# The last stores of an attention and feed-forward kernel: one transfer for each 128-row quarter, and the last quarter scaled in two halves

## The chip, the cores and the metric

The kernel runs on one core of a Trainium2 chip. The metric is the time of one execution in microseconds on the device; the median of several runs is compared. A core has a matrix engine (TensorE, PE in the profile), a vector engine (VectorE, DVE), a scalar engine (ScalarE, ACT), GpSimd (POOL) and SyncE (SP), which mainly issues transfers. Each engine runs its own instructions in order and waits on semaphores for the others. Transfers between the on-chip memory (SBUF) and the device memory (DRAM) are issued by SyncE, ScalarE or GpSimd and carried out by 16 DMA engines that all queues share. Matrix products are accumulated in PSUM, eight banks of 2 KB for each of 128 partitions; VectorE and ScalarE read them from there.

## The reference

Attention over 32 memory slots for 8 batches and 8 heads, then a bilinear feed-forward layer. Cut to what matters:

```python
# attention: q, k, v (8, 8, 576, 64), phi (8, 8, 576, 32)
a = softmax(phi, axis=2)
k_m = einsum('bhsm,bhsd->bhmd', a, k)
v_m = einsum('bhsm,bhsd->bhmd', a, v)
attn_out = softmax(q @ k_m.T / 8) @ v_m

# feed-forward: x (4608, 512), w_a, w_b (512, 1536), w_out (1536, 512)
x = attn_out.transpose(0, 2, 1, 3).reshape(4608, 512)
out = ((x @ w_a) * (x @ w_b)) @ w_out          # float32, (4608, 512)
```

## The kernel before, in words

The 4608 tokens are handled as 36 blocks of 128 rows; a block consists of two slots of 64 rows. A row of a slot is one token, and the tokens of one slot stand nine rows apart in the output (`out_rows`, with `NI` = 9 slots in a batch). Two neighbouring slots of one batch stand one row apart.

A long hand-written list, `PLAN`, sets the order in which the parts of the attention, the two upward products (`up_half`, which writes the products a * b into `ht`) and the downward product are recorded; each engine executes its instructions in that order. There is no scheduler behind it. The downward product with `w_out` is in `two_downs`: two blocks at a time, by Strassen's scheme (Winograd's form), with seven products of six matmuls each in place of eight. The sums of token blocks (`h_sums`, line 537) and of weight blocks (`w_sums`) are made beforehand by VectorE and GpSimd. A generator yields after each matmul, so that the plan can mix these steps with others; at the very end only they are left.

For the two blocks of one call there are two output tiles of 128 x 512 in SBUF, `o1` and `o2`. Each has a right half (columns 256 to 511) and a left half (columns 0 to 255), which gives four quarters. They become ready in this order:

1. `o1` right: product into bank `pv`, then `plus` (VectorE, line 564) scales it and adds `u2`
2. `o2` right: product into bank `py`, then `plus`
3. `o1` left: product into a bank of its own, `px`, then `plus`
4. `o2` left: product `a22` times `T4` into `py`, then only a scaling

`part` (ScalarE, line 560) makes the scaled partial sums `u1`, `u5` and `u2`.

The last call (`ends`, where `cidx` is `BLOCKS - 2`) differs from the others. The others scale the fourth quarter on ScalarE (line 604) and store each block whole, one transfer for each slot, from SyncE. The last call scales the fourth quarter on VectorE (line 602) and stores each quarter as soon as it is ready, in two transfers of 64 rows x 256 columns (64 KB, rows of 1 KB), one for each slot. `store` (lines 539 to 543) takes the two engines that issue them:

- `o1` right: both on GpSimd (line 583)
- `o2` right: SyncE and ScalarE (line 588)
- `o1` left: SyncE and ScalarE (line 595)
- `o2` left: SyncE and ScalarE (line 606)

An issue waits on its engine for the quarter that it sends, and blocks what stands behind it on that engine. After the last store the program ends: SyncE waits for the semaphores of all transfers, and a barrier of all engines follows.

Of the kernel before, what the change touches and what calls it, by code (L numbers as in the profile page):

```python
# [11 lines left out]
ALU = mybir.AluOpType  # L12
# [66 lines left out]
def kernel(  # L79
# [11 lines left out]
    nc = tc.nc  # L91
# [3 lines left out]
    d_model, d_ff = moe_w_a.shape  # L95
    NHP = H // 2
    NI = S // 64
# [408 lines left out]
    out_rows = out.rearrange("(b p i) f -> b i p f", b=B, i=NI)  # L506

    KH = NFF // 2
    NH = d_model // 2
    w_sums = wpool.tile([P, 4, KH, NH], F16, name="w_sums")  # L510

    def quarter(x, y):
        return wo_sb[:, KH * x:KH * (x + 1), NH * y:NH * (y + 1)]
# [8 lines left out]
    def tokens_of(cidx, x):  # L522
        pair, c = divmod(cidx, NI)
        return ht[:, KH * x:KH * (x + 1), P * c:P * (c + 1)]
# [13 lines left out]

    def store(o_sb, cidx, cs=slice(0, d_model), engines=(nc.sync, nc.sync)):
        pair, c = divmod(cidx, NI)  # L540
        for z in range(2):
            slot = 2 * c + z
            engines[z].dma_start(out=out_rows[2 * pair + slot // NI, slot % NI, :, cs], in_=o_sb[64 * z:64 * z + 64, cs])

    def two_downs(cidx):
        T1, T2, T3, T4 = (w_sums[:, x] for x in range(4))
        (a11, a12), (a21, a22) = ([tokens_of(cidx + y, x) for x in range(2)] for y in range(2))
        scale = 1.0 / (CS * CS)
        ends = cidx == BLOCKS - 2

        def products(po, lhs, rhs, first=False):
            for i in range(KH):
                nc.tensor.matmul(po, lhs[:, i], rhs[:, i], start=first and i == 0,  # L553
                                 stop=i == KH - 1, skip_group_check=not first)
                if i < KH - 1:
                    yield

        def part(po, name):
            x = ppool.tile([P, NH], F32, name=name)
            nc.scalar.mul(out=x, in_=po, mul=scale)  # L560
            return x

        def plus(o, po, x):
            nc.vector.scalar_tensor_tensor(out=o, in0=po, scalar=scale, in1=x, op0=ALU.mult, op1=ALU.add)

        o1, o2 = (opool.tile([P, d_model], F32, name="o_sb") for _ in range(2))
        y, ybank = banks.take([P, NH], F32, "py", hold=True)
        yield from products(y, a11, quarter(0, 0), True)
        u1 = part(y, "u1")
        yield  # L570
        v, vbank = banks.take([P, NH], F32, "pv", hold=True)
        S1, S2, S4, S3 = (h_sums[cidx][:, x] for x in range(4))
        yield from products(v, S1, T1, True)
        u5 = part(v, "u5")
        yield
        yield from products(y, S2, T2)
        u2 = part(y, "u2")
        yield
        yield from products(v, S4, quarter(1, 1))
        banks.free(vbank)  # L580
        plus(o1[:, NH:], v, u2)
        if ends:
            store(o1, cidx, slice(NH, d_model), (nc.gpsimd, nc.gpsimd))
        yield
        yield from products(y, S3, T3)
        plus(o2[:, NH:], y, u5)
        if ends:
            store(o2, cidx + 1, slice(NH, d_model), (nc.sync, nc.scalar))
        yield
        x, xbank = banks.take([P, NH], F32, "px", hold=True)  # L590
        yield from products(x, a12, quarter(1, 0), True)
        banks.free(xbank)
        plus(o1[:, :NH], x, u1)
        if ends:
            store(o1, cidx, slice(0, NH), (nc.sync, nc.scalar))
        else:
            store(o1, cidx)
        yield
        yield from products(y, a22, T4)
        banks.free(ybank)  # L600
        if ends:
            nc.vector.tensor_scalar(out=o2[:, :NH], in0=y, scalar1=scale, scalar2=None, op0=ALU.mult)
        else:
            nc.scalar.mul(out=o2[:, :NH], in_=y, mul=scale)
        if ends:
            store(o2, cidx + 1, slice(0, NH), (nc.sync, nc.scalar))
        else:
            store(o2, cidx + 1)
        yield
# [3 lines left out]
    def downs():  # L613
        for cidx in range(0, BLOCKS, 2):
            yield from two_downs(cidx)
# [19 lines left out]
    for x in PLAN.split():  # L635
# [17 lines left out]
        elif x[0] in "hg":  # L653
            n, y = arg.split(".")
# [34 lines left out]
```

## Time and profile before

| what | value |
|---|---|
| median of 3 runs | 236.83 us (236.87, 236.83, 236.38) |
| the profiled execution's own time | 236.16 us |
| its span on the core | 234.4 us |
| TensorE clock granted | 0.996 of full speed |
| transfers in the span | 38420 packets, 37.27 MB |
| stores of 128 KB, issue to landing (median of 68) | 2.6 us |
| stores of 64 KB, issue to landing (median) | SyncE 2.1 us, ScalarE 2.6 us, GpSimd 2.3 us |
| GpSimd's issue of a 64 KB store | 0.58 to 0.59 us |
| SyncE's issue of a 64 KB store | 0.47 us |
| ScalarE's issue of a 64 KB store | 0.55 to 0.73 us |

The span is the time from the first to the last instruction on the core; the execution's own time holds a little more around it. The rows of busy time by slice show TensorE at 9 tenths or more nearly all the way, up to the last of 40 slices:

```profile
PE   7887899999999999999999999999999999999993
...
DMA  6999999999999998597997589853170323122155
GB/s 230 239 252 203 207 207 206 229 235 257 213 224 289 202 240 196 130 229 118 190 183 169 111 137 227 164 110 77 26 166 3 92 50 92 45 48 51 41 137 134
```

One digit is the busy share of a slice of 5.9 us in tenths. The last slice holds the end of the last products, all the quarter stores and the closing of the program. Lines of the profile read as: line of the code, engine, operation, tile written, tile read, shapes, count, and then busy time in us and the mean of one in ns. In a timeline the first two numbers are start and duration in us.

### The profile page before, as it was taken

Reading aid. Unit: us, or ns where it says so; the run is one execution under the profiler, and the core shown is the slowest. Engines: PE = TensorE matmul, PEld = TensorE weight load, DVE = VectorE, ACT = ScalarE, POOL = GpSimd, SP = SyncE. Lnnn points to the kernel's source line nnn. Section 1 sums busy time; section 2 is a strip of 40 time slices with the busy share of each in tenths; the row PEclk is TensorE's granted clock in tenths of the full one; section 3 lists DMA queues with packets and bytes.
Section 4 is the critical chain, followed back from the end, with each engine's and each line's share of the span. In section 5 each row is a group of like instructions: output and inputs, shape, how many; then the busy total and the mean of one; then the engine's idle time right before and its main releaser. Section 6 shows DMA issues by size and latency. Waiting matters only on the chain.

```text
span 234.4 us, 7699 instructions
## 1 busy us (share of the span) xinstructions
PE 224.6 (96%) x3059; PEld 169.9 (72%) x3059; DVE 185.0 (79%) x450; ACT 152.3 (65%) x398; POOL 120.0 (51%) x109
## 2 busy tenths in 40 slices
PE   7887899999999999999999999999999999999993
PEld 4533456788868886777777778888668878888882
DVE  3533889999998889868797998977978897776862
ACT  2228699875778797766687786556786865465330
POOL 7577423795779525908947982324066002325051
PEclk9999999999999999999999999999999999999998
DMA  6999999999999998597997589853170323122155
GB/s 230 239 252 203 207 207 206 229 235 257 213 224 289 202 240 196 130 229 118 190 183 169 111 137 227 164 110 77 26 166 3 92 50 92 45 48 51 41 137 134
DMA packets 38420, 37.27 MB, mean 159 GB/s; under 512 B 14672, under 2 KB 32464, under 8 KB 38384
## 3 DMA queue, kind: packets, MB, share of 16 engines
q0 software_dynamic: 19248, 23.14, 53.6%
q1 hardware_dynamic: 18624, 12.85, 23.8%
q10 hardware_dynamic: 512, 0.79, 1.0%
q8 instruction: 24, 0.39, 0.7%
q14 instruction: 12, 0.10, 0.1%
HBM read 42.47 MB, written 9.44 MB: 221 GB/s over the span
## 4 chain that ended last, share of the span: by engine, by line
PE 77%; DMA 17%; POOL 3%; issue 1%; DVE 0%; POOLq 0%
PE py L553 19%; PE pa L624 18%; PE pb L624 18%; DMA kv_sb<-in_v_dram 12%; PE pv L553 10%; PE pva L449 5%; PE px L553 5%; DMA phi_sb<-in_phi_dram 5%; PE pkv L286 2%; POOL q_sb L150 1%; PE pscore L380 1%; POOL h_sums L537 1%; POOL phi_sb L138 0%; PE pk L345 0%; POOL kv_sb L145 0%
## 5 line engine op out<-in xcount | busy, mean ns | idle before, releaser
L631 DVE TENSOR_TENSOR ht<-a_sb,pb 128x288 f16<-128x288 f16 x192 | 79.9, 447 | 18.7 <-PE pb L624 9.0
L628 ACT CAST a_sb<-pa 128x288 f16<-128x288 f32 x192 | 71.5, 408 | 34.8 <-PE pa L624 28.9
L624 PEld LDWEIGHTS <-vab 128*128 128x128 f16 x768 | 73.5, 98 | 19.6 <-issue 4.5
L624 PE MATMUL pa<-A,vab 128*128 128x288 f16 x384 | 69.9, 286 | 0.9 <-DVE A L414 0.8
L624 PE MATMUL pb<-A,vab 128*128 128x288 f16 x384 | 70.5, 286 | 0.0
L553 PEld LDWEIGHTS <-h_sums 128*128 128x128 f16 x432 | 41.6, 98 | 10.4 <-issue 3.2
L537 POOL TENSOR_TENSOR h_sums<-ht 128x768 f16<-128x768 f16 x17 | 27.9, 1646 | 29.9 <-DVE ht L631 29.9
L553 PEld LDWEIGHTS <-ht 128*128 128x128 f16 x324 | 31.3, 98 | 6.3 <-issue 1.1
L553 PE MATMUL py<-w_sums,h_sums 128*128 128x256 f16 x216 | 35.2, 273 | 0.0
L462 ACT CAST vab<-pva 128x512 f16<-128x512 f32 (+1 forms) x60 | 31.6, 568 | 4.8 <-PE pva L449 4.1
L537 POOL TENSOR_TENSOR h_sums<-h_sums,ht 128x768 f16<-128x768 f16 x12 | 19.7, 1642 | 27.3 <-DVE h_sums L537 15.9
L462 DVE CAST vab<-pva 128x512 f16<-128x512 f32 (+1 forms) x44 | 26.8, 633 | 3.4 <-PE pva L449 3.1
L537 POOL TENSOR_TENSOR h_sums<-ht,h_sums 128x768 f16<-128x768 f16 x9 | 15.0, 1664 | 17.6 <-DVE h_sums L537 17.2
L260 ACT ACTIVATE exp_sb<-phi_sb 128x576 f16<-128x576 f32 x16 | 11.0, 698 | 12.4 <-DMA phi_sb<-in_phi_dram 12.4
L560 ACT ACTIVATE u<-py 128x256 f32<-128x256 f32 x36 | 14.1, 392 | 6.9 <-PE py L553 6.5
L553 PE MATMUL py<-wo_sb,ht 128*128 128x256 f16 x108 | 18.5, 273 | 0.0
L553 PE MATMUL pv<-wo_sb,h_sums 128*128 128x256 f16 x108 | 18.5, 273 | 0.0
L553 PE MATMUL px<-wo_sb,ht 128*128 128x256 f16 x108 | 18.4, 273 | 0.0
L553 PE MATMUL pv<-w_sums,h_sums 128*128 128x256 f16 x108 | 17.7, 273 | 0.0
L553 PE MATMUL py<-w_sums,ht 128*128 128x256 f16 x108 | 17.0, 272 | 0.0
L269 DVE STREAM_TRANSPOSE qT<-q_sb 128x288 f32<-128x288 f32 x32 | 14.0, 458 | 1.8 <-DMA q_sb<-in_q_dram 1.6
L211 PE MATMUL pw<-warm 128*128 128x128 f16 (+1 forms) x67 | 12.2, 334 | 1.3 <-DVE warm L180 1.3
(67 smaller groups left out, 241.4 us busy)
## 6 DMA issues: line engine op xcount, KB each, us to landing
out_dram<-o_sb SPq DMA_DIRECT2D x68, 128.0 KB, 2.6
phi_sb<-in_phi_dram POOLq DMA_DIRECT2D x8, 576.0 KB, 7.6
kv_sb<-in_v_dram POOLq DMA_DIRECT2D x8, 576.0 KB, 10.1
kv_sb<-in_k_dram POOLq DMA_DIRECT2D x7, 576.0 KB, 12.7
q_sb<-in_q_dram POOLq DMA_DIRECT2D x6, 576.0 KB, 8.3
wo_sb<-in_moe_w_out_dram POOLq DMA_DIRECT2D x6, 256.0 KB, 15.8
q_sb<-in_q_dram POOLq DMA_DIRECT2D x4, 288.0 KB, 9.9
wa_sb<-in_moe_w_a_dram POOLq DMA_DIRECT2D x2, 512.0 KB, 14.5
```

The source lines that it names most:

```text
L211: nc.tensor.matmul(pw[:, :cols], warm[:, :P], warm[:, :cols], start=True, stop=True)
L260: nc.scalar.activation(out=t["exp"][:, 2 * z:2 * z + 2, :, :], in_=phis[b][:, 2 * z:2 * z + 2, :].rearrange("p c (i m) -> p c i m", m=M), ...
L269: nc.vector.transpose(out=t["qT"][:, hp, :].bitcast(F32), in_=qs[b][:, hp, :].bitcast(F32))
L286: nc.tensor.matmul(t["pkv"][g][0][32 * j:32 * j + 32, 0:n], t["exp"][64 * r:64 * r + 64, hp, i, :], kvs[b][64 * r:64 * r + 64, 0:3 - given ...
L449: nc.tensor.matmul(t["pva", lo, z][g][0][32 * j:32 * j + 32, 0:hi - lo], t["kvT"][64 * r:64 * r + 64, 4 + g, M * j:M * j + M], w_sbs[z][64 ...
L462: engine_copy(out=vabs[b][z][:, g, lo:hi], in_=pva[:, 0:hi - lo])
L537: engine.tensor_tensor(out=out, in0=in0, in1=in1, op=op)
L553: nc.tensor.matmul(po, lhs[:, i], rhs[:, i], start=first and i == 0, stop=i == KH - 1, skip_group_check=not first)
L560: nc.scalar.mul(out=x, in_=po, mul=scale)
L624: nc.tensor.matmul(ps, vabs[b][x][:, g, P * i:P * (i + 1)], attn[b][:, g, HALF * hf:HALF * (hf + 1)], start=(g == 0), stop=(g == 1))
L628: nc.scalar.copy(out=a_sbs[b, i, hf], in_=ps)
L631: nc.vector.tensor_tensor(out=ht[:, i, t0:t0 + HALF], in0=a_sbs.pop((b, i, hf)), in1=ps, op=ALU.mult)
```

## The change

`store` gets a form for one engine: where `engines` has one entry, it sends the whole 128 rows of a column range in one transfer, whose DRAM side is two slots of 64 rows. The first three quarters of the last call use it: GpSimd for `o1` right, ScalarE for `o2` right, SyncE for `o1` left. The fourth quarter is still stored in two transfers of 64 rows from SyncE and ScalarE. It is scaled by two instructions: VectorE takes columns 0 to 127 and ScalarE columns 128 to 255, both from the same PSUM bank `py`.

```diff
     def store(o_sb, cidx, cs=slice(0, d_model), engines=(nc.sync, nc.sync)):
         pair, c = divmod(cidx, NI)
+        if len(engines) == 1:
+            b, i = 2 * pair + 2 * c // NI, 2 * c % NI
+            engines[0].dma_start(out=out_rows[b, i:i + 2, :, cs], in_=o_sb[:, cs])
+            return
         for z in range(2):
...
         if ends:
-            store(o1, cidx, slice(NH, d_model), (nc.gpsimd, nc.gpsimd))
+            store(o1, cidx, slice(NH, d_model), (nc.gpsimd,))
...
         if ends:
-            store(o2, cidx + 1, slice(NH, d_model), (nc.sync, nc.scalar))
+            store(o2, cidx + 1, slice(NH, d_model), (nc.scalar,))
...
         if ends:
-            store(o1, cidx, slice(0, NH), (nc.sync, nc.scalar))
+            store(o1, cidx, slice(0, NH), (nc.sync,))
...
         if ends:
-            nc.vector.tensor_scalar(out=o2[:, :NH], in0=y, scalar1=scale, scalar2=None, op0=ALU.mult)
+            nc.vector.tensor_scalar(out=o2[:, :NH // 2], in0=y[:, :NH // 2], scalar1=scale, scalar2=None, op0=ALU.mult)
+            nc.scalar.mul(out=o2[:, NH // 2:NH], in_=y[:, NH // 2:], mul=scale)
         else:
             nc.scalar.mul(out=o2[:, :NH], in_=y, mul=scale)
```

## The prediction

> **What bounds the kernel now.** I read the page from the top, then the timeline of the last five microseconds, then the transfers of that stretch, because the diff touches nothing before it (the order of the built program's instructions is the same on every engine up to the last stores).
>
> ```profile
> span 234.4 us, 7699 instructions
> PE 224.6 (96%) x3059; PEld 169.9 (72%) x3059; DVE 185.0 (79%) x450; ACT 152.3 (65%) x398; POOL 120.0 (51%) x109
> ...
> PE 77%; DMA 17%; POOL 3%; issue 1%; DVE 0%; POOLq 0%
> ```
>
> TensorE is the bound until its last product; the change adds and removes no matmul, so nothing is to be had there. What can move is the tail behind the last product. Its timeline (start, duration, engine, line, tiles):
>
> ```profile
> 229.38 1.16 POOL L543 DMA_DIRECT2D out_dram<-o_sb  x2 [2.36 <-DVE o_sb L564]
> ...
> 229.74 1.80 SPq L543 DMA_DIRECT2D out_dram<-o_sb  x3
> 229.74 2.04 ACTq L543 DMA_DIRECT2D out_dram<-o_sb  x3
> 229.76 0.82 PE L553 MATMUL py<-w_sums,ht 128*128 128x256 f16 x6
> 229.94 0.42 DVE L564 SCALAR_TENSOR_TENSOR o_sb<-px,u 128x256 f32<-128x256 f32 x1 [0.23 <-PE px L553]
> 230.61 0.42 DVE L602 TENSOR_SCALAR o_sb<-py 128x256 f32<-128x256 f32 x1 [0.25 <-PE py L553]
> ```
>
> The last product ends at 230.58, VectorE scales it from 230.61 to 231.03, and SyncE and ScalarE issue the last two stores; by the instructions of the o_sb tile SyncE's starts at 231.1 and ScalarE's at 231.2, behind its own earlier store. From there to 234.4 no engine computes. The transfers between 230.2 and 233.2, in 40 slices of 0.075 us:
>
> ```profile
> DMA  0000799203799891299938678999969986851000
> ...
> DMA packets 544, 0.52 MB, mean 175 GB/s; under 512 B 128, under 2 KB 512, under 8 KB 544
> ...
> q1 hardware_dynamic: 240, 0.20, 22.8%
> q10 hardware_dynamic: 240, 0.20, 22.2%
> q0 software_dynamic: 64, 0.13, 18.6%
> ```
>
> Three things are to be seen. First, the delay from an issue to its first packet: GpSimd's store of 229.38 shows at 230.50, SyncE's of 229.74 at 230.88, so about 1.15 us. Second, the last packet ends in the slice before 232.97, and the span ends 1.40 us later (landing, SyncE's closing waits, the final barrier): a fixed tail. Third, the 128 packets under 512 bytes are the completions of the eight stores of the tail, 16 each. Each queue q1 (SyncE) and q10 (ScalarE) has 240 = 3 x (64 + 16): a store of 64 rows is 64 packets of 1 KB in 16 shares of four, one share for each of the 16 DMA engines, and each share reports once.
>
> **The change, part by part.**
>
> *Scaling in halves.* Not at once: in the built program ScalarE's multiply waits for VectorE's semaphore, at the count that VectorE's own half raises, and has no wait on TensorE left. So the halves run one after the other. Prices of halves:
>
> ```profile
> L393 ACT ACTIVATE E<-pscore 128x288 f16<-128x288 f32 x32 | 11.1, 416 | 1.6 <-PE pscore L380 1.5
> ...
> L560 ACT ACTIVATE u<-pv 128x256 f32<-128x256 f32 x18 | 7.0, 390 | 4.9 <-PE pv L553 4.7
> ...
> L318 DVE TENSOR_SCALAR rep<-pkv,rphi 128x256 f16<-128x256 f32 x12 | 5.8, 484 | 0.4
> ...
> L318 DVE TENSOR_SCALAR rep<-pkv,rphi 128x128 f16<-128x128 f32 x12 | 4.1, 342 | 0.0
> ```
>
> VectorE saves 484 - 342 = 142 ns on 128 columns, so its half takes 424 - 142 = 0.28 us. ScalarE has no row of 128 columns; 26 ns for 32 columns gives 390 - 104 = 0.29 us (bounds: 0.2, half of 390, and 0.39). With two handovers of about 0.04 us (230.58 to 230.61 is one) the result is ready at 230.61 + 0.28 + 0.04 + 0.29 + 0.04 = 231.26. Before, SyncE's last store started at 231.1 and ScalarE's at 231.2: the last stores start 0.05 to 0.2 us later. Queued behind the waiting multiply on ScalarE is only its own last store; SyncE's last store waits for the same multiply. The Trainium skill speaks against the idea too: "PSUM — Partial Sum Buffer", section "PSUM bank collisions raise a hardware error", says that no two engines may access one bank at the same partitions at once, even to read; no row of this case has two readers of one bank.
>
> *Fewer issues.* GpSimd loses one issue of 0.58 us, SyncE one of 0.47, ScalarE one of 0.55 to 0.73. I cost all three at nothing: GpSimd's ended at 230.55, the removed SyncE issue at 230.2, and ScalarE's remaining one (229.74 to 230.3) is over before VectorE's half ends at 230.90, which covers it. Without that cover it would cost at most its 0.55.
>
> *One transfer in place of two.* This is the term that decides. The three new stores write 128 rows, and on the DRAM side their outermost dimension is 2 (two slots), then 64 rows. Every store before has 64 rows outermost on both sides, and those 64 are what the rows above show cut into 16 shares. No row shows how an outermost dimension of 2 is cut. From one side it is still 16 engines; then nothing changes but the 0.05 to 0.2 us. From the other it is cut like the 64, along its outermost dimension, and 2 gives two shares: two engines with 64 rows each. I take the second end, because all stores that the trace shows are cut evenly along that dimension (64 packets, 16 completions, four rows each).
>
> The price of a row on one engine, from a stretch in which nearly all engines are busy (columns at the end: clock, DMA share, GB/s):
>
> ```profile
> 232.00:232.50 0.50, 0.00 (x0) 0.00 (x0) 0.00 (x0) 0.00 (x0) 0.00 (x0) 1.00 0.87 281
> ```
>
> 0.87 x 16 engines x 0.5 us = 6.96 us of engine time for 281 GB/s x 0.5 us = 137 rows of 1 KB: 51 ns a row. Other bounds: q1 and q10 above, 22.5% x 16 x 3.0 us = 10.8 us for 192 rows, 56 ns; SyncE's 2 KB rows alone (203 to 206 us: 37.8% of 48 us for 0.26 MB) 71 ns for a KB; from below 44 ns (one of the highest slices of 0.05 us between 231 and 233 us, 369 GB/s; 16 x 1024 / 369).
>
> ScalarE's store (issued 229.74) and SyncE's (230.39) would then both lie on the same two engines (no row tells the engines of one queue from the other's), 64 rows of each on each, and the two last stores still put four rows each there, behind them: 136 rows. First packet 229.74 + 1.15 = 230.89; 136 x 51 ns = 6.94 us; last packet 237.83; plus the tail of 1.40: 239.23. Against 234.37 that is **+4.9 us**. The later scaling disappears under it: the last rows stand in a queue until 237.8 anyway. So the sum is 0 (TensorE) + 0 (issues) + 0 (scaling, covered; 0.05 to 0.2 if the cover is gone) + 4.9.
>
> The profiled execution took 236.16 us, the median is 236.83 and the runs reach from 236.38 to 236.87: the profiled one is 0.7 below the median, and 1.8 us of it lie around its span. 236.16 + 4.9 = 241.0 is a profiled execution; for the median I add to 236.83: **241.7 us**. With 44 ns it is 240.8, with 71 ns 244.4.
>
> The Trainium skill, "DMA: Bandwidth & Descriptors", section "Why a DMA increments its semaphore by 16 and not by 1", has a rule for this: a transfer uses the largest number of engines up to 16 that divides the outermost dimension (other than 1) on both sides, and SyncE's and ScalarE's transfers take the lowest-numbered ones. For 128 and 2 that is two engines, the same two for both queues; by it the sum is the one above, and by the row of 16 completions alone it would be about 237.0. It adds that GpSimd's transfers sometimes get 16 all the same. No run here has shown it yet.
>
> **Rivals.**
>
> *GpSimd's store on the same two engines (slower still).* Its 128 KB would add 64 rows to each: at 51 ns 3.3 us, at q0's own price (18.6% of 48 us for 128 KB, 70 ns) 4.5. Time 245.0 to 246.2. For it: it has the same shape. Against it: its packets are cut by a different maker (16 data packets a store of 4 KB each, where the others have 64 of 1 KB), so its cut need not follow.
>
> *The two queues on different pairs (less slow).* Then SyncE's store decides: 230.39 + 1.15 + 68 x 51 ns = 235.01, plus 1.40 = 236.4, +2.1: 238.9. Against it: nothing in the trace separates the queues' engines; each store uses all 16.
>
> *Sixteen engines (not slower).* The place is the cut of the new stores. With k engines each has 256/k + 8 rows from 230.89 on, and today's last packet is at 232.97: (256/k + 8) x 51 ns stays below 2.08 us from k = 8 up. Then only the scaling is left: +0.05 to +0.2, about 237.0, within 0.2% (0.47 us, about what a measurement of this kernel can tell from no change). For it: every row of the trace has 16 completions. A gain: fewer completions and GpSimd's half out 0.58 us earlier; the last stores still start later than today, and the shortest landing among the o_sb stores is 2.0 us where the medians are 2.1 (SyncE) and 2.6 (ScalarE), so a gain stays within a few tenths of a microsecond.
>
> *The change does not do what it says.* True of "at once", which is priced above; if the halves did overlap, 0.15 us would be saved, too little to show.
>
> **How the numbers follow.** Two shared engines 0.60 (241.7; own range 240.8 to 244.4); GpSimd's on them as well 0.18 (245.6); separate pairs 0.06 (238.9); eight engines or more 0.16 (237.0), of which 0.11 within 0.2%, 0.02 slower, 0.03 faster. Slower 0.60 + 0.18 + 0.06 + 0.02 = 0.86. The range 238.7 to 246.4 takes the first three and leaves out the last and a few hundredths at the top.
>
> **What would show it.** After the change, the slices after 230.9 should show a DMA share near 2 of 16 for some six microseconds, the 128 KB stores of SyncE and ScalarE should land 6 to 8 us after their issue, and packets under 512 bytes should be fewer than 16 for each of them. VectorE's half should read about 0.28 us and ScalarE's should start after its end. A share near 0.8 that ends by 233 would prove the cut wrong; a long tail at a share well above 2 of 16, the price of a row.

## The result and the profile after

The changed kernel takes 245.07 us (median of 6 runs, 243.13 to 245.68) against 236.81 us (6 runs, 235.65 to 237.42): a ratio of 1.034, 95% interval 1.030 to 1.038, some 8 us slower. Ratios, here and below, are worked out from the single runs without those in which the core was in a slower state, and need not be the quotient of the two medians. The time lies inside the range on record, but not near its likeliest case (241.7): it is that of the first rival.

The page after the change: TensorE's busy time is nearly what it was (225.5 us against 224.6), and the span is 9.5 us longer.

```profile
span 243.9 us, 7695 instructions
PE 225.5 (92%) x3059; PEld 170.1 (70%) x3059; DVE 185.1 (76%) x450; ACT 152.5 (63%) x399; POOL 119.6 (49%) x108
...
PE 71%; DMA 19%; POOL 3%; issue 1%; DVE 1%; ACT 0%; SPq 0%; POOLq 0%
```

The timeline of its end (start, duration, engine, line):

```profile
230.58 0.89 POOL L543 DMA_DIRECT2D out_dram<-o_sb  x1 [2.37 <-DVE o_sb L568]
...
230.94 1.15 ACTq L543 DMA_DIRECT2D out_dram<-o_sb  x1
230.96 0.81 PE L557 MATMUL py<-w_sums,ht 128*128 128x256 f16 x6
231.14 0.42 DVE L568 SCALAR_TENSOR_TENSOR o_sb<-px,u 128x256 f32<-128x256 f32 x1 [0.23 <-PE px L557]
231.59 0.61 SPq L543 DMA_DIRECT2D out_dram<-o_sb  x1
231.82 0.29 DVE L606 TENSOR_SCALAR o_sb<-py 128x128 f32<-128x128 f32 x1 [0.25 <-PE py L557]
232.21 0.28 ACT L607 ACTIVATE o_sb<-py 128x128 f32<-128x128 f32 x1 [2.63 <-DMA out_dram<-o_sb]
232.51 0.52 SPq L547 DMA_DIRECT2D out_dram<-o_sb  x1
232.52 0.56 ACTq L547 DMA_DIRECT2D out_dram<-o_sb  x1
```

The last product ends at 231.78, and the span ends at 243.85. I call the stretch between them the tail: 12.07 us, where it was 3.80. The tail grew by 8.27 us, which is the whole difference of the medians (8.26). The other 1.2 us of the longer span lie before the last product and are not of the change: in the profiles below, all alike up to there, that product ends anywhere from 230.5 to 233.2.

The halves do run one after the other (VectorE's ends at 232.11, ScalarE's starts at 232.21). But the last two stores are issued by 233.1, and what follows is some nine microseconds of transfers. The transfers from 232 to 243 us, in slices of 0.275 us, and one stretch of two microseconds (last columns: clock, DMA share, GB/s):

```profile
DMA  2232110041798212121201111111111111100000
...
DMA packets 692, 0.53 MB, mean 48 GB/s; under 512 B 276, under 2 KB 660, under 8 KB 692
...
q1 hardware_dynamic: 210, 0.20, 8.5%
q10 hardware_dynamic: 210, 0.20, 6.7%
q0 software_dynamic: 272, 0.13, 5.5%
...
out_dram<-o_sb SPq DMA_DIRECT2D x1, 64.0 KB, 10.3
out_dram<-o_sb ACTq DMA_DIRECT2D x1, 64.0 KB, 9.9
```

```profile
238.00:240.00 2.00, 0.00 (x0) 0.00 (x0) 0.00 (x0) 0.00 (x0) 0.00 (x0) 0.50 0.13 46
```

A DMA share of 0.13 is two engines of sixteen (0.125). And the counts say the same: q10 had 240 = 3 x (64 + 16) packets in the tail before; now it has 210 = 128 + 64 rows, 16 completions of ScalarE's last store and **two** completions of its single store. SyncE's q1 has the same 210. The last stores, of 64 rows on all sixteen engines, land 10 us after their issue: four of their rows stand on each of the two crowded engines, behind the others. A row of 1 KB there costs 0.13 x 16 / 46 GB/s = 46 ns.

### The profile page after: what moved, and what is told of

It reads as the page before. It is cut to its first block, busy times and chain, and to the rows that moved or that the text cites. A ratio compares the mean times of both kernels' runs of the same rounds, so it can differ in the third digit from the quotient of the medians.

```text
span 243.9 us, 7695 instructions
## 1 busy us (share of the span) xinstructions
PE 225.5 (92%) x3059; PEld 170.1 (70%) x3059; DVE 185.1 (76%) x450; ACT 152.5 (63%) x399; POOL 119.6 (49%) x108
## 4 chain that ended last, share of the span: by engine, by line
PE 71%; DMA 19%; POOL 3%; issue 1%; DVE 1%; ACT 0%; SPq 0%; POOLq 0%
PE pa L629 17%; PE py L557 17%; PE pb L629 17%; DMA kv_sb<-in_v_dram 12%; PE pv L557 9%; DMA phi_sb<-in_phi_dram 5%; PE pva L449 5%; PE px L557 4%; PE pkv L286 2%; DMA A<-E 2%; PE pscore L380 1%; POOL q_sb L150 1%; POOL h_sums L537 1%; DMA out_dram<-o_sb 1%; POOL phi_sb L138 0%
## 5 line engine op out<-in xcount | busy, mean ns | idle before, releaser
L211 PE MATMUL pw<-warm 128*128 128x128 f16 (+1 forms) x67 | 12.9, 348 | 1.3 <-DVE warm L180 1.3
```

The source lines that it names most:

```text
L211: nc.tensor.matmul(pw[:, :cols], warm[:, :P], warm[:, :cols], start=True, stop=True)
```

## The experiments

Ten kernels were run. Each is a version of the kernel before or of the changed one; times are medians, and ratios are against runs of the kernel before on the same chip, with 95% intervals. "Tail" is read from the one profiled execution of each.

**1. The halves alone.** The kernel before with only the scaling of the last quarter changed:

```diff
-            nc.vector.tensor_scalar(out=o2[:, :NH], in0=y, scalar1=scale, scalar2=None, op0=ALU.mult)
+            nc.vector.tensor_scalar(out=o2[:, :NH // 2], in0=y[:, :NH // 2], scalar1=scale, scalar2=None, op0=ALU.mult)
+            nc.scalar.mul(out=o2[:, NH // 2:NH], in_=y[:, NH // 2:], mul=scale)
```

> The last quarter scaled in halves, all quarters stored in two transfers of 64 rows as before. Theory (the cut of the new stores on two engines costs everything, the halves run in a row but cost 0.05 to 0.2 us): 236.8 to 237.1 us, ScalarE's half starts after VectorE's ends. Rival (the halves and their wait carry a good part of the 8.3 us): 238 or more.

237.16 us against 237.31; ratio 1.0015 (0.9978 to 1.0052). In time nothing can be told; the tail of the profile is 4.13 us, 0.33 longer (one profile of each), and nothing points to the rival's 238. Its timeline shows why that is more than the 0.05 to 0.2 expected:

```profile
230.48 1.38 ACTq L543 DMA_DIRECT2D out_dram<-o_sb  x2
...
231.35 0.29 DVE L602 TENSOR_SCALAR o_sb<-py 128x128 f32<-128x128 f32 x1 [0.25 <-PE py L553]
231.96 0.28 ACT L603 ACTIVATE o_sb<-py 128x128 f32<-128x128 f32 x1 [2.84 <-DVE o_sb L602]
232.27 0.50 ACTq L543 DMA_DIRECT2D out_dram<-o_sb  x1
```

VectorE's half ends at 231.64, but ScalarE's starts at 231.96: with two transfers for each quarter ScalarE has one of the second quarter and one of the third to issue, and the later one takes until 231.86. The idle time is put down to VectorE, since its semaphore came last in the list; the issue in ScalarE's own queue is what it waited for.

**2. The single transfers alone.** The changed kernel with the last quarter scaled whole by VectorE (the edit above, backwards).

> The three first quarters in one transfer each, the last quarter scaled whole by VectorE as before. Theory (the cut costs everything; the later scaling is hidden behind queued rows): 244.8 to 245.3 us, the same as the changed kernel. Rival (the halves carry a part): clearly below, 244 or less.

246.09 us (244.76 to 246.60), ratio 1.035 (1.029 to 1.041); tail 11.56 us. The median lies above the 244.8 to 245.3 expected, on a chip on which the kernel before takes 237.31; the ratio is that of the changed kernel. So the transfers alone carry the loss. Without the halves the one profiled tail is 0.5 us shorter, but the runs show nothing won back.

**3. GpSimd's quarter in two again.** The changed kernel with one call edited:

```diff
-            store(o1, cidx, slice(NH, d_model), (nc.gpsimd,))
+            store(o1, cidx, slice(NH, d_model), (nc.gpsimd, nc.gpsimd))
```

> The changed kernel, but GpSimd's quarter goes out in two transfers of 64 rows again; ScalarE's and SyncE's stay single. Theory A (GpSimd's single store lies on the same two DMA engines as the others and takes their time): 2.7 to 4.3 us less than the changed kernel, 240.8 to 242.4, near the 241.7 forecast. Rival B (GpSimd's store lies on other engines and does not matter; the rows of the hardware queues cost more than the 51 ns assumed): 244.5 to 245.3, no change.

242.73 us (242.01 to 244.57), ratio 1.023 (1.016 to 1.030); tail 9.48 us, 2.59 less than the changed kernel's. The interval only touches that of the changed kernel (1.030 to 1.038), but on this chip all four runs (up to 244.57) lie below all four of experiment 2 (from 244.76). So theory A: GpSimd's store takes time from the two engines of the others. The packet records of the changed kernel show it directly: a 4 KB packet of GpSimd's ends at 233.86, a 1 KB row of ScalarE's single store runs from 233.85 to 233.90, GpSimd's next packet from 233.90 to 234.06, the next row from 234.05 to 234.10, and so on in turn (times to within 0.01 us). What is left is what the prediction's likeliest case described, two hardware stores on two engines, and it stands 5.4 us over the kernel before (3.7 to 7.0 by the interval; 5.7 by the tails), where 4.9 were predicted.

**4. GpSimd's quarter alone.** The kernel before, with the edit of experiment 3 the other way round.

> The kernel before, but GpSimd's quarter goes out in one transfer; all else as before. Theory (its 128 rows lie on two DMA engines, 16 packets of 4 KB each, as the 4.3 us of its packets in the changed kernel's profile say): it lands 5 to 6 us after its issue and ends the program 1 to 2.5 us later, 238 to 239.3. Rival (it is spread over 16 engines and was slow only because the others were in its way): 236.6 to 237.0.

239.89 us (239.70 to 240.97), a little above the range expected; ratio 1.011 (1.004 to 1.018); tail 6.29 us. The stores of this kernel from 230 us on (count, KB each, and the median time from issue to landing in us):

```profile
out_dram<-o_sb SPq DMA_DIRECT2D x3, 64.0 KB, 4.6
out_dram<-o_sb ACTq DMA_DIRECT2D x3, 64.0 KB, 4.9
...
out_dram<-o_sb POOLq DMA_DIRECT2D x1, 128.0 KB, 5.8
```

GpSimd's lands 5.8 us after its issue, as expected. The other two lines show what it does to its neighbours: the six stores of SyncE and ScalarE are untouched, 64 rows over 16 engines, and yet they land after 4.6 and 4.9 us in place of 2.1 and 2.6. By the packet records all but the last four completions of each of the two queues are there by 235.7, and the last four come at 236.0 to 236.6: two of each of the last two stores, as they would behind GpSimd's packets on two engines. Since these stores use all 16 engines, this does not say which two; the records under experiment 3 do, for the changed kernel. It is not the whole delay either: the other completions, too, are later than before (the last of them 4.0 us after the last product, where before all had come after 2.4), and why is left open.

**5. ScalarE's quarter alone.** The kernel before with only `o2` right in one transfer, from ScalarE.

> The kernel before, but ScalarE's quarter (o2 right) goes out in one transfer; the others in two, the last quarter scaled whole. Theory (one such store alone occupies two engines: first packet 1.8 us after the issue as in the run with GpSimd in two, then 64 + 8 rows at 42 to 51 ns on each): 1.6 to 2.3 us slower than before, about 238.5 to 239.5. Rival (only two such stores on the same engines hurt; alone it is hidden): 236.8 to 237.5.

239.46 us (238.77 to 240.32), ratio 1.0105 (1.0072 to 1.0138), 2.5 to 2.7 us; tail 6.61 us: slower as the theory says, and by more than its 1.6 to 2.3. I had counted 64 + 8 rows on each of the two engines; with four 64-row stores of SyncE and ScalarE beside it there are 64 + 16, which at 46 ns is 0.4 us more.

**6. The same size, another cut.** The single transfers of experiment 2, but to a spare tensor in DRAM, whose 128 rows lie at one even distance; these three quarters do not reach the output.

```diff
+    CUT = 128
+    spare = nc.dram_tensor("spare", (CUT, P // CUT + (CUT < P), 3, 2 * d_model), F32, kind="Internal").ap()
...
-            engines[0].dma_start(out=out_rows[b, i:i + 2, :, cs], in_=o_sb[:, cs])
+            to = spare[:, :P // CUT, len(sent), cs]
+            if CUT == P:
+                to = to.rearrange("a b f -> (a b) f")
+            engines[0].dma_start(out=to, in_=o_sb[:, cs])
```

> The three single stores of 128 rows x 1 KB, but to a spare DRAM tensor whose rows lie at one even distance, so that the outermost dimension is 128 on both sides; these three quarters do not reach the output. Theory (only the outermost dimension of 2 costs): the stores land in 2 to 3 us with 16 completions each and the time is that of the kernel before, 236.5 to 237.5. Rival (128 rows in one transfer cost as such, in the issue or in the queue): 239 or more.

236.66 us, ratio 0.9968 (0.9938 to 0.9997); tail 3.81 us, that of the kernel before. Packets and stores of its end:

```profile
q10 hardware_dynamic: 224, 0.20, 15.1%
q0 software_dynamic: 48, 0.13, 8.9%
...
spare<-o_sb POOLq DMA_DIRECT2D x1, 128.0 KB, 2.2
spare<-o_sb ACTq DMA_DIRECT2D x1, 128.0 KB
spare<-o_sb SPq DMA_DIRECT2D x1, 128.0 KB, 1.8
```

224 packets are 128 + 64 rows and 16 + 16 completions. So one transfer of 128 rows costs nothing as such: the same bytes in rows of the same size, issued by the same engines at the same point of the program, land in 2 us (GpSimd's and SyncE's; the profile gives no landing for ScalarE's) when the outermost dimension is 128. ScalarE's issue takes 0.36 us there (by the instructions of its o_sb tile), and 1.15 with the outermost dimension of 2.

**7. Half of each row.** Experiment 2, but the single stores send the first 128 columns of their 256; half of these three quarters does not reach the output.

```diff
+            cs = slice(cs.start, cs.start + NH // 2)
             engines[0].dma_start(out=out_rows[b, i:i + 2, :, cs], in_=o_sb[:, cs])
```

> The run with single stores and the scaling undone, but the three single stores send only 128 of their 256 columns (rows of 512 bytes, the same count of rows); half of these three quarters does not reach the output. If a row on an engine is priced by its bytes: half of the 8 us is gone, 240.5 to 242. If it is priced by its count: 244.5 or more.

240.46 us (240.34 to 240.95), ratio 1.011 (1.006 to 1.016); tail 7.38 us. A stretch in which only the pair works:

```profile
235.90:237.10 1.20, 0.00 (x0) 0.00 (x0) 0.00 (x0) 0.00 (x0) 0.00 (x0) 0.50 0.14 41
```

Two engines move 41 GB/s in rows of 512 bytes, where they moved 46 in rows of 1 KB: 2 x 512 / 41 = 25 ns a row. The price goes by the bytes of a row, nearly, and not by the count of rows.

**8 and 9. Eight groups, four groups.** Experiment 6 with `CUT = 8` and `CUT = 4`: the spare tensor has 8 groups of 16 rows, or 4 of 32, with a gap behind each group, so that two levels remain. These three quarters do not reach the output.

> As the run with an outermost dimension of 128, but the spare tensor is cut into 8 groups of 16 rows, so that the outermost dimension is 8 on the DRAM side; these three quarters do not reach the output. Theory (the number of engines is that of the outermost dimension, here 8, and from 8 up it is hidden): 8 completions from each of SyncE's and ScalarE's single stores, 236.8 to 237.9. Rival (any two-level DRAM side falls to two engines): 244 or more.

> As the run with an outermost dimension of 8, but 4 groups of 32 rows; these three quarters do not reach the output. Theory (engines = outermost dimension; all three stores on the same four): 5 updates of the semaphore for SyncE's and ScalarE's (12 at once and 4), 72 rows at 42 to 51 ns and eight 4 KB packets on each of four engines, 2 to 3.5 us slower than before, 238.7 to 240.3. Rival (powers below 8 all fall to two engines): 244 or more.

Eight: 237.65 us, ratio 1.0032 (0.9997 to 1.0067), tail 4.45. Four: 240.25 us, ratio 1.016 (1.011 to 1.021), tail 7.45; that is 3.8 us over its 236.48, a little more than the 2 to 3.5 expected. The row of ScalarE's queue in each of the two:

```profile
q10 hardware_dynamic: 216, 0.20, 12.8%
```

```profile
q10 hardware_dynamic: 212, 0.20, 13.2%
```

216 = 128 + 64 + 16 + 8 and 212 = 128 + 64 + 16 + 4: eight completions and four. With 16 and two from above:

| outermost dimension on the DRAM side | completions of ScalarE's single store | ratio to the kernel before | tail, us |
|---|---|---|---|
| 128 | 16 | 0.9968 (0.9938 to 0.9997) | 3.81 |
| 8 | 8 | 1.0032 (0.9997 to 1.0067) | 4.45 |
| 4 | 4 | 1.016 (1.011 to 1.021) | 7.45 |
| 2 (experiment 2) | 2 | 1.035 (1.029 to 1.041) | 11.56 |

Eight groups also take apart two things that experiment 6 changed together. Their DRAM side still has two levels, and ScalarE's issue still takes 1.18 us (1.11 with four groups, 1.15 with two), yet the tail is only 0.65 us longer than before. So the two levels as such are worth that at most, by one profile of each; what comes on top with four groups and with two goes with the number of engines. One step stays mixed: no run writes the spare tensor in two groups, so the last line differs from the one above it in the place that is written as well.

**10. A try for less than before.** ScalarE's last store in the kernel before waits 0.16 us behind its earlier one, so the second transfer of the third quarter went to GpSimd:

```diff
-            store(o1, cidx, slice(0, NH), (nc.sync, nc.scalar))
+            store(o1, cidx, slice(0, NH), (nc.sync, nc.gpsimd))
```

> The kernel before with one edit: the second 64-row transfer of the third quarter is issued by GpSimd in place of ScalarE, whose queue is then free when the last quarter is ready (its last store waited 0.16 us behind the one before). Theory: the last store starts 0.16 us earlier and the tail behind the last product is 3.6 to 3.8 us; the time differs from before by less than the measurement tells, 236.3 to 237.3. Rival (GpSimd's packets hold up the last stores): 237.5 or more.

237.49 us against 236.48, ratio 1.0031 (1.0002 to 1.0060): a miss, if anything slower; tail 4.21. ScalarE's last store did start with SyncE's, both at 231.02, but the last landing came 2.9 us after the last product, against 2.8 before. And the closing got longer: of the program's last line GpSimd's queue has this row (duration least, median, longest; first and last start):

```profile
L684 POOLq DRAIN  x3: 46/93/3381, 230.6 to 234.5; - x3
```

The longest, 3.38 us, ends at 233.97, after SyncE has seen all landings (233.7), and the barrier waits for it. In the kernel before the same drain ended at 233.4, ahead of SyncE (233.6). No version that writes the whole output and is faster than the kernel before was found.

## Why the prediction was right, and where it was off

*What decides.* Right, and shown: the single transfers carry the whole loss (experiments 1 and 2), and in them the outermost dimension of 2 (6, 8 and 9 vary it; against experiment 2 they also write to another place). Of the two ends between which the trace before left the choice, the one cut along the outermost dimension is the true one; the rule of the Trainium skill that stood beside it ("DMA: Bandwidth & Descriptors", section "Why a DMA increments its semaphore by 16 and not by 1") agrees with all four counts of 16, 8, 4 and 2.

*Which case.* The step that failed is the choice among the cases. The likeliest, 0.60, put nothing down for GpSimd's store; the rival with it on the same two engines, 0.18, is what happened: 245.0 to 246.2 were worked out for it and 245.07 measured. The argument against that rival, that another maker of packets need not cut in the same way, was wrong in fact: in the changed kernel GpSimd's packets and ScalarE's rows take turns on the same engines (experiment 3). So the Trainium skill's remark, in the same section, that GpSimd's transfers sometimes get 16 engines all the same did not hold for this shape. GpSimd's term is 2.6 us (the tails of experiment 3 and the changed kernel), below the 3.3 to 4.5 of the rival's sum: a 4 KB packet of GpSimd's takes 0.16 us when nothing is in its way (packet records), so the sixteen on each engine are 2.5 us, 40 ns a KB and not 51 to 70. That the rival's sum came so close is in part luck, since this term was too large and the next one too small.

*The two hardware stores.* 4.9 us predicted, 5.4 by experiment 3's ratio and 5.7 by its tail. The row price was nearly right: from the first packet of ScalarE's single store in experiment 3 (232.12 by the packet records) to the last of all (239.27) are 7.15 us for 136 rows, 53 ns, where 51 were taken; alone, a pair is at 46. Too small was the delay ahead of it: 1.15 us from issue to first packet was read from GpSimd's and SyncE's stores, and this one took 1.8 (230.31 to 232.12). ScalarE's own first store in the kernel before, issued at 229.74, has its first packet at 231.39, 1.65 us later; reading that queue would have given most of the difference.

*The halves.* Right that they are no overlap, and right, as far as the runs can tell, that they hide under the queue. By themselves they cost 0.33 us of tail where 0.05 to 0.2 were worked out; the missing part is ScalarE's own issue, which I costed as covered, and of which there is one more with two transfers for each quarter (experiment 1). In the changed kernel that cover was thin: the issue ends at 232.09, beside VectorE's half at 232.11.

*Sixteen engines as a rival.* Its limit, no loss from eight engines up, stands at the edge of what was measured: 1.0032 (0.9997 to 1.0067) and 0.65 us of tail for eight, so the runs cannot tell eight engines from no loss, and whether the 0.65 us belong to the eight engines or to the longer issue is open.

*What would show it.* The share near 2 of 16 was there, the completions were two, but the last stores landed after some ten microseconds, and the single ones had their last completions 10.7 us after their issues (packet records), and not after six to eight: GpSimd's part came on top.

## What to carry to other kernels

Before two transfers are made one, look at the outermost dimension on both sides of the new one: here it set the number of DMA engines, and a 2 in that place cost 8 us where 128 cost nothing, for the same bytes. A store that is cut badly also holds up good ones, because their rows stand behind it on the same few engines, so the loss shows in transfers that the edit does not touch. And two halves of one PSUM bank given to two engines may be put in a row: read in the built program what each half waits for, and count the engine's own issues among it.

## What was not expected of the hardware

The issue of a store does not go by its size: ScalarE's took 0.36 us for 128 rows at one even distance (experiment 6), 0.50 to 0.76 for 64 rows, and 1.11 to 1.18 for 128 rows in two levels, whether in 2, 4 or 8 groups. So it is the second level, and not the number of engines, that goes with the long issue. Why is left open.

GpSimd's queue shows its number of engines in another way. Beside the 32 packets of 4 KB of its single store and 16 completions, the packet records have 224 packets of 16 bytes with two groups, 96 with four, 32 with eight and none with 128. These are 14 x 16, 12 x 8 and 8 x 4: as many as one for each data packet of an engine on each engine that has no data. That they are this is an inference from the counts.

GpSimd's closing drain ended 0.9 us after its last store had landed, in the kernel before (landing 232.51, drain 233.42), in experiment 10 (233.02 and 233.97) and in experiment 4 (236.30 and 237.18); a late store on GpSimd therefore ends later than its landing says.
